# Two-layer attention decode: K and V in transfers of 32 KiB rows out of one planned arena

## The chip, the cores and the metric

One core of a Trainium2 chip runs the program. The metric is the device time of one execution in microseconds (us), here the median of three runs. TensorE (PE in the rows) multiplies, VectorE (DVE), ScalarE (ACT) and GpSimd (POOL) do the small work, and SyncE (SP) issues all transfers from HBM into the on-chip memory SBUF, which has 128 partitions. The transfers of one queue are carried by 16 DMA engines.

## The reference

Two different blocks are applied alternately, twice, to one token `x` of 512 elements. All is float32.

```python
def _A_ref(x, k_cache, v_cache, wq, wo):          # 32 heads, 4096 keys, 128 per head
    q = (x @ wq) as [1, 32, 1, 128]
    scores = einsum("bhqd,bhkd->bhqk", q, k_cache) * 128 ** -0.5
    p = softmax(scores)
    o = einsum("bhqk,bhkd->bhqd", p, v_cache)
    return o as [1, 1, 4096] @ wo

def _B_ref(x, w1, b1, w2, b2):                    # 512 -> 1376 -> 512
    return gelu(x @ w1 + b1) @ w2 + b2

x = x + _A_ref(layernorm(x), K, V, wq, wo)
x = x + _B_ref(layernorm(x), w1, b1, w2, b2)
x = x + _A_ref(layernorm(x), K, V, wq, wo)        # the same K, V and weights again
x = x + _B_ref(layernorm(x), w1, b1, w2, b2)
```

K and V have 64 MiB each, wq and wo 8 MiB each, w1 and w2 some 2.7 MiB each. Both layers read the same ones, and SBUF holds about a sixth of them, so nearly all of it is read twice.

## The kernel before

The 32 heads go in eight groups of four, one head of a group for each quadrant of the PE array. The 4096 keys of a group are cut into eight chunks of 512. A chunk of K (or of V) of one group is a tile of 128 partitions by 2048 elements: 8 KiB per partition, 1 MiB in all, and one transfer. wq and wo of a group have the same size.

Layer 0 takes the groups from 0 to 7, layer 1 from 7 to 0. For each group the program writes down, in this order:
- `scores`: eight chunks of K are fetched and multiplied with the queries (L158); 
- `query_block` and `queries`: wq of the next group is fetched and its queries are made (L145 to L152);
- `softmax` (L162 to L179);
- `values`: eight chunks of V are fetched and multiplied (L184);
- `head_out`: wo of the group is fetched, and the output of the heads is multiplied with it and added up in `pW` (L197).

After the eighth group `mlp` multiplies with w1 (L206), applies the GELU (L215 to L220) and multiplies with w2 in eleven blocks of 32 hidden units (L225). The mean and the variance of the layer norms come from small products with `negmean` (L126).

All tiles come from one pool, `ring`, of 25 buffers of 8 KiB per partition (`SLOTS`). `fetch` takes the next buffer and issues the transfer on SyncE's queue. A buffer is loaded anew when the engines have finished with its last content. In layer 0 the last 22 tiles (`KEPT`: K, V, wq and wo of group 7, wq and wo of group 6, and two chunks of V of group 6) stay in their buffers and are not fetched again in layer 1. A further chunk of V is copied to four free banks of PSUM (`pK`) and back (L78, L69). So layer 1 begins with work that needs no transfer.

Each transfer signals one of eight semaphores in turn, and SyncE issues a transfer when the one eight places before it has landed, so eight are in flight. The first three quarters of w1 (`w1_t`, 16,512 bytes of each partition, which lie 22,016 bytes apart in HBM) have a place of their own and are loaded once, before chunk 4 of the last V of layer 0. The rest of w1 (`w1_3`, rows of 1,376 bytes) and w2 in three parts go through the ring behind the last wo, in both layers. The last values of a layer are multiplied in the order 4, 0, 1, 2, 3, 5, 6, 7 (`ORDER`).

Of the kernel before, what the change touches and what calls it, by code (L numbers as in the profile page):

```python
# [12 lines left out]
F32 = mybir.dt.float32  # L13
# [14 lines left out]
SLOTS = 25           # streaming buffers of 8 KiB per partition  # L28
KEPT = 22            # buffers that stay filled from the first layer to the second
W1_AT = 4            # chunk of the last values before which w1 is loaded  # L30
MEAN_AT, VAR_AT = 0, 1   # parts of w1 whose products the mean and the variance follow
W2_PARTS = (3, 4, 4)     # blocks of 32 hidden units in each part of w2
ORDER = (4, 0, 1, 2, 3, 5, 6, 7)   # of the products with the last values: without
                                   # pauses, so that the tensor engine's clock is up
# [3 lines left out]
def decode_layers(ctx: ExitStack, tc: tile.TileContext, x, k, v, wq, wo, w1, b1, w2, b2, out):  # L38
    nc = tc.nc
    const = ctx.enter_context(tc.tile_pool(name="const", bufs=1))  # L40
    ring = ctx.enter_context(tc.tile_pool(name="ring", bufs=SLOTS))
# [8 lines left out]

    last = G - 1
    kept = [("k", last, c) for c in range(C)] + [("v", last, c) for c in range(C)]
    kept += [("wq", last), ("wo", last), ("wq", last - 1), ("wo", last - 1)]
    kept += [("v", last - 1, c) for c in range(C)]
    in_psum = kept[KEPT]
    kept = set(kept[:KEPT])
    held = {}

    def fetch(layer, what, *at):
        key = (what, *at)  # L60
        if key in held:
            return held.pop(key)
        src = dict(k=k, v=v, wq=wq, wo=wo)[what]
        for i in at:
            src = src[i]
        t = ring.tile([P, J, 512], F32, name="stream")
        if layer == 1 and key == in_psum:
            for j in range(J):
                nc.scalar.copy(t[:, j, :], pK[j])  # L69
            return t  # L70
        if key == ("wo", 0 if layer else last):
            for i in (0, 2):
                nc.sync.dma_start(t[:, i : i + 2, :], src[:, i : i + 2, :])
        else:
            nc.sync.dma_start(t, src)  # L75
        if layer == 0 and key == in_psum:
            for j in range(J):
                nc.scalar.copy(pK[j], t[:, j, :])  # L78
        if layer == 0 and key in kept:
            held[key] = t  # L80
        return t

# [3 lines left out]
    wq_next = fetch(0, "wq", 0)  # L86
    nc.sync.dma_start(b1c, b1)
    nc.sync.dma_start(b2c, b2)
    w1_t = ctile("w1_t", 3, J, FJ)

# [7 lines left out]
    # PSUM: four banks of products, and four that keep one more tile for the second layer.  # L98
    # Rows that no product writes are zero once and for all.
# [15 lines left out]
    # x and ones beside it: a product with both gives x W and the sums of W's columns.  # L115
# [85 lines left out]
    def mlp(xs, s, w1_3, w2_t):  # L201
        xb = small("xb", 4)
        nc.gpsimd.tensor_tensor(xb, xs[:, :, 0], b2c, op=ALU.add)  # L203
        for c in range(4):
            for j in range(J):
                nc.tensor.matmul(pH[32 * j : 32 * j + 2, :FJ], xs[:, c, :], w1_t[:, c, j, :] if c < 3 else w1_3[:, j, :FJ],  # L206
                                 start=(c == 0), stop=(c == 3))
# [113 lines left out]
```

## Time and profile before

| | |
|---|---|
| time of three runs | 701.38 us median (701.29 to 702.08) |
| span of the profiled execution, first to last instruction | 699.0 us |
| queue of SyncE | 287.19 MB, busy for 99.2% of 16 engines' span |
| mean rate | 412 GB/s |
| TensorE, weight load, VectorE, ScalarE busy | 63%, 12%, 11%, 3% |
| mean granted clock of TensorE | 0.73 |
| chain that ended last | DMA 86%, PE 10%, DVE 2% |

The span is 2.4 us shorter than the median of the runs, which also hold what lies ahead of the first and behind the last instruction. The share of the queue says how long its packets were under way on the 16 engines; it doesn't say that they ran at their best rate. The chain of waits is followed back from the last instruction; a piece of it that reads "DMA" is the time from the issue of a transfer to its landing, in which the transfers ahead of it in the queue are moved too. The granted clock is a share of TensorE's full 2.4 GHz, with 1.2 GHz (0.5) as the lower level.

### The profile page before, as it was taken

How to read it: one execution, taken by the hardware profiler on the slowest of the kernel's cores; microseconds unless marked ns; L12 is line 12 of the kernel's file. 1: busy time of each engine (PE TensorE's matmuls, PEld its weight loads, DVE VectorE, ACT ScalarE, POOL GpSimd, SP SyncE). 2: the span in 40 equal slices, each digit the busy share in tenths (PEclk: the TensorE clock that was granted, in tenths of full speed). 3: DMA queues.
4: the chain of work that ended last, by engine and by line, in shares of the span. 5: the costliest groups of instructions: out<-in, count | busy, mean ns of one | idle time of the engine just before them, and what ended most of it. 6: DMA issues, size and time to landing. Idle time of an engine off the chain costs nothing.

```text
span 699.0 us, 7892 instructions
## 1 busy us (share of the span) xinstructions
PE 440.4 (63%) x3440; PEld 87.3 (12%) x3440; DVE 77.8 (11%) x314; ACT 19.7 (3%) x43; POOL 3.5 (1%) x17
## 2 busy tenths in 40 slices
PE   4566666557656764666537887666767566665545
PEld 1010100001001010010003231101001001010012
DVE  2100101001001010010102120101001000010012
ACT  0100000000000000010000100000000000000000
POOL 0000000000000000000000000000000000000000
PEclk9676677876676568666659999765566756667768
DMA  8999999999999999999998999999999999999995
GB/s 340 420 422 421 420 421 420 422 421 420 421 421 422 420 421 421 420 422 420 424 418 327 417 421 420 421 421 421 421 422 420 423 420 423 420 421 423 421 418 228
DMA packets 41123, 287.70 MB, mean 412 GB/s; under 512 B 4992, under 2 KB 6016, under 8 KB 6784
## 3 DMA queue, kind: packets, MB, share of 16 engines
q1 hardware_dynamic: 41088, 287.19, 99.2%
q8 instruction: 27, 0.44, 0.3%
q14 instruction: 8, 0.07, 0.0%
HBM read 287.17 MB, written 0.00 MB: 411 GB/s over the span
## 4 chain that ended last, share of the span: by engine, by line
DMA 86%; PE 10%; DVE 2%; issue 1%; SPq 0%; ACT 0%; ACTq 0%; DVEq 0%
DMA stream<-in_v 40%; DMA stream<-in_k 27%; DMA stream<-in_wq 12%; DMA stream<-in_wo 6%; PE pO L184 5%; PE pS L158 2%; PE pB L197 1%; PE pA L225 1%; PE pB L206 1%; DMA stream<-in_w 1%; DVE wide L189 1%; SPq L75 0%; DVE mx L162 0%; PE pA L145 0%; DVE on L194 0%
## 5 line engine op out<-in xcount | busy, mean ns | idle before, releaser
L158 PE MATMUL pS<-stream,zq 128*8 128x512 f32 x1024 | 191.4, 837 | 90.9 <-DMA stream<-in_k 90.9
L184 PE MATMUL pO<-stream,pt 128*4 128x512 f32 x1024 | 173.5, 797 | 91.4 <-DMA stream<-in_v 86.2
L184 PEld LDWEIGHTS pO<-stream,pt 128*4 128x4 f32 x1024 | 21.8, 92 | 224.9 <-DMA stream<-in_v 155.4
L158 PEld LDWEIGHTS pS<-stream,zq 128*8 128x8 f32 x1024 | 18.6, 89 | 244.3 <-DMA stream<-in_k 232.2
L162 DVE TENSOR_REDUCE mx<-pS 128x1 f32<-128x512 f32 x16 | 11.1, 692 | 300.4 <-PE pS L158 300.4
L189 DVE STREAM_TRANSPOSE wide<-pO 128x512 f32<-128x512 f32 x16 | 11.5, 717 | 259.9 <-PE pO L184 259.9
L197 PE MATMUL pB<-stream,on 128*1 128x128 f32 x512 | 25.4, 361 | 20.0 <-DVE on L194 18.5
L171 PE MATMUL pO<-ident,wide 128*128 128x128 f32 x64 | 15.9, 396 | 31.2 <-ACT wide L169 31.2
L145 PE MATMUL pA<-stream,xs 128*2 128x128 f32 x512 | 24.4, 341 | 12.1 <-DMA stream<-in_wq 11.3
L169 ACT ACTIVATE wide<-pS,bias,sc 128x512 f32<-128x512 f32 x16 | 12.4, 777 | 580.2 <-DVE zq L152 485.7
L197 PEld LDWEIGHTS pB<-stream,on 128*1 128x1 f32 x512 | 14.3, 103 | 47.8 <-DVE on L194 43.5
L145 PEld LDWEIGHTS pA<-stream,xs 128*2 128x2 f32 x512 | 14.4, 100 | 35.4 <-DMA stream<-in_wq 28.4
L171 PEld LDWEIGHTS pO<-ident,wide 128*128 128x128 f32 x64 | 10.2, 195 | 39.0 <-ACT wide L169 35.7
L225 PE MATMUL pA<-stream,gelu_g 128*1 128x128 f32 x176 | 8.5, 372 | 4.5 <-DVE gelu_g L220 4.3
L225 PEld LDWEIGHTS pA<-stream,gelu_g 128*1 128x1 f32 x176 | 5.9, 111 | 7.7 <-DVE gelu_g L220 5.6
L150 DVE STREAM_TRANSPOSE wide<-pA 128x128 f32<-128x128 f32 x16 | 5.1, 316 | 11.5 <-PE pA L145 11.4
L175 DVE STREAM_TRANSPOSE mt<-ls 128x32 f32<-128x32 f32 x16 | 3.4, 211 | 17.5 <-ACT wide L169 17.5
L206 PE MATMUL pB<-w_t,xs 128*2 128x344 f32 x48 | 4.3, 450 | 1.4 <-DVE xs L120 1.4
L173 DVE COPY pt<-pO 128x128 f32<-128x128 f32 x16 | 4.5, 281 | 3.6 <-PE pO L171 3.6
L203 POOL TENSOR_TENSOR xb<-xs,b2c 128x4 f32<-128x4 f32 x2 | 0.4, 198 | 668.7 <-DVE xs L120 668.7
L166 DVE TENSOR_SCALAR mb<-m,nsc 128x8 f32<-128x8 f32 x16 | 3.7, 230 | 0.5
L194 DVE TENSOR_SCALAR on<-o,rl 128x4 f32<-128x4 f32 x16 | 3.7, 229 | 0.6
(68 smaller groups left out, 57.2 us busy)
## 6 DMA issues: line engine op xcount, KB each, us to landing
stream<-in_k SPq DMA_DIRECT2D x120, 1024.0 KB, 19.8
stream<-in_v SPq DMA_DIRECT2D x117, 1024.0 KB, 19.8
stream<-in_wq SPq DMA_DIRECT2D x14, 1024.0 KB, 19.8
stream<-in_wo SPq DMA_DIRECT2D x12, 1024.0 KB, 19.8
stream<-in_w SPq DMA_DIRECT2D x4, 1024.0 KB, 16.1
w_t<-in_w SPq DMA_DIRECT2D x1, 2064.0 KB, 22.3
stream<-in_wo SPq DMA_DIRECT2D x4, 512.0 KB, 19.3
stream<-in_w SPq DMA_DIRECT2D x2, 768.0 KB, 16.1
```

What stands on the lines that cost most here:

```text
L145: nc.tensor.matmul(pQ[32 * j : 32 * j + 2, :], xs[:, c, :], wt[:, c, P * j : P * (j + 1)], start=(c == 0), stop=(c == 3))
L150: nc.vector.transpose(qt, pQ)
L158: nc.tensor.matmul(pS[32 * j : 32 * j + C, :], z[:, j, C - 1 - c : 2 * C - 1 - c], kt[:, j, :], start=(c == 0), stop=(c == C - 1))
L162: nc.vector.tensor_reduce(mx[:, 0:1], pS, axis=AX.X, op=ALU.max)
L169: nc.scalar.activation(p, pS, AF.Exp, bias=bias[:, 0:1], scale=sc, accum_out=ls[:, 0:1])
L171: nc.tensor.transpose(pT[:, b].rearrange("p j r -> p (j r)"), p[:, P * b : P * (b + 1)], ident)
L173: nc.vector.tensor_copy(pt, pT[:, :, :, :C].rearrange("p b j c -> p j c b"))
L184: nc.tensor.matmul(pO[32 * j : 32 * j + 4, :], pt[:, j, c, :], vt[:, j, :], start=(i == 0), stop=(i == C - 1))
L189: nc.vector.transpose(ot[:, :512], pO)
L197: nc.tensor.matmul(pW[32 * j : 32 * j + 1, :], on[:, d : d + 1], wt[:, d, P * j : P * (j + 1)], start=first and d == 0, stop=final and d == 3)
L206: nc.tensor.matmul(pH[32 * j : 32 * j + 2, :FJ], xs[:, c, :], w1_t[:, c, j, :] if c < 3 else w1_3[:, j, :FJ], start=(c == 0), stop=(c == 3))
L225: nc.tensor.matmul(pM[32 * j : 32 * j + 1, :], g[:, c : c + 1], part[:, i, P * j : P * (j + 1)], start=(c == 0), stop=(c == FB - 1))
```

## The change

The ring is replaced by one tile, `arena`, of 27 places of 8 KiB per partition (216 KiB), and the program says for each transfer where in it the data goes (`load`). Every load is kept in the order of the program.

- K and V come in halves of four chunks: 128 rows of 32 KiB, 4 MiB per transfer. In HBM a half is stored so that a partition's four chunks are one run. The halves go round six blocks of four places in layer 0 and five in layer 1. Only the last V of each layer has its second half in four single chunks (`LAST`), and the first halves of layer 1 come in smaller pieces.
- wo and wq share one tensor `w` of two rows, in which wo of a group lies beside wq of a neighbour: one transfer of 128 rows of 16 KiB brings wo of this group and wq of the next into `PAIR`. The rows lie 64 KiB apart in HBM. The queries of the next group are therefore made after `head_out`, no longer before the softmax.
- w1 and w2 are loaded behind wo at the end of layer 0, each in two parts, to `HELD` and `SPARE`; the parts in `HELD` stay there, and layer 1 loads those in `SPARE` alone. wo of group 7 is a single load of 8 KiB rows.
- Kept from the first layer are K and V of group 7, wq and wo of group 7, and four chunks of V of group 6 (one by way of PSUM): 22 tiles. wq and wo of group 6 are fetched again. wq and two chunks of K of group 6 are loaded to `SPARE` when the products of layer 0 with w1 and w2 have been made.

```diff
+U = 512
+NC = 4 * U
+BLOCK = 4 * NC
+RING1, RING2 = 6, 5
+SPARE = 19 * NC
+HELD = 22 * NC
+PAIR = 25 * NC
+ARENA = 27 * NC
+W1H, W2A, W2B = 2 * FJ * J, 6 * U, 5 * U
+LAST = ((0, 4), (4, 5), (5, 6), (6, 7), (7, 8))
+HALVES = ((0, 4), (4, 8))
...
-        t = ring.tile([P, J, 512], F32, name="stream")
...
+    arena = const.tile([P, ARENA], F32, name="arena")
+    def load(at, src):
+        t = arena[:, at : at + src.shape[-1]]
+        tc.keep_in_program_order(nc.sync.dma_start(t, src))
         return t
...
+    def of_w(first, n):
+        row, i = first
+        return w[row][:, NC * i : NC * (i + n)]
...
+    def part(src, g, a, b):
+        h = a // 4
+        return src[g, h][:, NC * (a - 4 * h) : NC * (b - 4 * h)]
...
+    def stream(what, g, pieces, homes=None):
+        nonlocal block
+        src = k if what == "k" else v
+        for a, b in pieces:
+            if homes is not None:
+                at = homes[a]
+            else:
+                at = block * BLOCK + (a % 4) * NC
+                if b % 4 == 0:
+                    block = (block + 1) % ring
+            t = load(at, part(src, g, a, b))
+            for c in range(a, b):
+                here[what, g, c] = chunk(t, c - a)
+                yield c, here[what, g, c]
...
-            for c in range(C):
-                scores(z, c, fetch(layer, "k", g, c))
-            if not final:
-                wt = fetch(layer, "wq", order[n + 1])
...
+            if layer == 1 and n == 0:
+                tiles = [(c, here["k", g, c]) for c in range(C)]
+            elif layer == 1 and n == 1:
+                tiles = [(c, here["k", g, c]) for c in range(2)]
+                tiles += list(stream("k", g, ((2, 4), (4, 8)), {2: 0, 4: 2 * NC}))
+            else:
+                tiles = stream("k", g, HALVES)
+            for c, t in tiles:
+                scores(z, c, t)
...
             pt, rl = softmax(sc, nsc)
...
-                    if final and layer == 0 and len(vt) == W1_AT:
-                        nc.sync.dma_start(w1_t, w1[:, :3])
...
+            elif final:
+                tiles = dict(stream("v", g, LAST))
+                for i, c in enumerate(ORDER):
+                    values(i, pt, tiles[c], c)
...
+            elif final:
+                wo_t = chunk(load(PAIR + NC * layer, of_w(wo_at(g), 1)))
+                if layer == 0:
+                    load(HELD, w1[:, :W1H])
+                load(SPARE, w1[:, W1H:])
+                if layer == 0:
+                    load(HELD + W1H, w2[:, :W2A])
+                load(SPARE + W1H, w2[:, W2A:])
+            else:
+                t = load(PAIR, of_w(wo_at(g) if layer == 0 else wq_at(g - 1), 2))
+                wo_t, wq_next = (chunk(t, i) for i in ((0, 1) if layer == 0 else (1, 0)))
+            head_out(rl, wo_t, first, final)
+            if not final and not (layer == 1 and n == 0):
+                for c in range(4):
+                    query_block(c, xs, wq_next)
+                z = queries(n + 1, negm)
...
         if layer == 0:
             xs, s = set_x(of_32(mt, 4), 0.5, xb)
+            g = G - 2
+            wq_first = wq_next
+            wq_next = chunk(load(SPARE, of_w(wq_at(g), 1)))
+            for c in range(2):
+                here["k", g, c] = chunk(load(SPARE + NC * (c + 1), part(k, g, c, c + 1)))
```

Three places show how the order of the instructions changes. First SyncE's queue in a steady group of layer 0 (group 1), before and after; `in_w` is the common tensor of wq and wo in the changed kernel.

```order
L75 DMA stream<-in_k 128x2048 x8
L75 DMA stream<-in_wq 128x2048
L75 DMA stream<-in_v 128x2048 x8
L75 DMA stream<-in_wo 128x2048
L75 DMA stream<-in_k 128x2048 x8
```

```order
L62 DMA arena<-in_k 128x8192 x2
L62 DMA arena<-in_v 128x8192 x2
L62 DMA arena<-in_w 128x4096
L62 DMA arena<-in_k 128x8192 x2
L62 DMA arena<-in_v 128x8192 x2
```

Eighteen transfers of 1 MiB per group have become four of 4 MiB and one of 2 MiB, and wq has moved from between K and V to behind V.

Second, SyncE's queue from the last V of layer 0 into layer 1, with the semaphores that a transfer waits for (`DMAHW` are landings of earlier transfers, `PE` products that must be done). Here `in_w` is also the short name of w1 and w2, which the sizes tell apart. Before:

```order
L75 DMA stream<-in_v 128x2048 [waits DMAHW2_49,PE_49]
L73 DMA stream<-in_wo 128x1024 [waits DMAHW3_49,PE_49]
L73 DMA stream<-in_wo 128x1024 [waits DMAHW4_49]
L269 DMA stream<-in_w 128x4x344 [waits DMAHW5_49,PE_49]
L273 DMA stream<-in_w 128x1536 [waits DMAHW6_49,PE_49]
L273 DMA stream<-in_w 128x2048 [waits DMAHW7_49,PE_49]
L273 DMA stream<-in_w 128x2048 [waits DMAHW5_49,DMAHW0_49,PE_49]
L75 DMA stream<-in_k 128x2048 [waits DMAHW6_49,DMAHW1_49,PE_49]
L75 DMA stream<-in_k 128x2048 [waits DMAHW7_49,DMAHW2_49,PE_49]
```

And in the changed kernel:

```order
L62 DMA arena<-in_v 128x2048 [waits DMAHW5_49,PE_49]
L62 DMA arena<-in_w 128x2048 [waits DMAHW6_49,PE_49]
L62 DMA arena<-in_w 128x2752 [waits DMAHW7_49]
L62 DMA arena<-in_w 128x2752 [waits DMAHW0_49,Activation_49]
L62 DMA arena<-in_w 128x3072 [waits DMAHW1_49]
L62 DMA arena<-in_w 128x2560 [waits DMAHW2_49]
L62 DMA arena<-in_w 128x2048 [waits DMAHW3_49,DMAHW0_49,PE_49]
L62 DMA arena<-in_k 128x2048 [waits DMAHW4_49,DMAHW2_49,PE_49]
L62 DMA arena<-in_k 128x2048 [waits DMAHW5_49,PE_49]
L62 DMA arena<-in_k 128x4096 [waits DMAHW6_49,PE_49]
L62 DMA arena<-in_k 128x8192 [waits DMAHW7_49,PE_49]
```

All of w1 and w2 now stands behind the last wo, its parts wait for no product, and the first loads of layer 1 (wq, then K in pieces of 1, 1, 2 and 4 MiB) are the next that do.

Third, TensorE at the edge between groups 0 and 1, before (`L197` is the product with wo, `L145` the queries, `L158` the scores, `L184` the values):

```order
L158 MATMUL pS<-stream,zq_97 8x512 x32
L145 MATMUL pA<-stream,xs 2x128 x16
L171 MATMUL pO<-ident,wide 128x128 x4
L184 MATMUL pO<-stream,pt 4x512 x32
L197 MATMUL pB<-stream,on 1x128 x16
L158 MATMUL pS<-stream,zq_98 8x512 x32
```

And in the changed kernel, where the lines of the same products are L156, L143, L169, L182 and L195:

```order
L156 MATMUL pS<-arena,zq_91 8x512 x32
L169 MATMUL pO<-ident,wide 128x128 x4
L182 MATMUL pO<-arena,pt 4x512 x32
L143 MATMUL pA<-arena,xs 2x128 x13
L195 MATMUL pB<-arena,on 1x128 x16
L143 MATMUL pA<-arena,xs 2x128 x3
L156 MATMUL pS<-arena,zq_92 8x512 x32
```

The queries of the next group have moved from ahead of the transposes of the softmax to both sides of the product with wo.

## Rows read from the trace of the kernel before

**Rows 1.** The page: busy time, rate in 40 slices, packets, queue.
```profile
PE 440.4 (63%) x3440; PEld 87.3 (12%) x3440; DVE 77.8 (11%) x314; ACT 19.7 (3%) x43; POOL 3.5 (1%) x17
...
GB/s 340 420 422 421 420 421 420 422 421 420 421 421 422 420 421 421 420 422 420 424 418 327 417 421 420 421 421 421 421 422 420 423 420 423 420 421 423 421 418 228
DMA packets 41123, 287.70 MB, mean 412 GB/s; under 512 B 4992, under 2 KB 6016, under 8 KB 6784
...
q1 hardware_dynamic: 41088, 287.19, 99.2%
```

**Rows 2.** Chain that ended last: start, duration in us, what.
```profile
16.82 21.19 DMA stream<-in_v
...
38.03 19.88 DMA stream<-in_k
...
256.80 21.37 DMA stream<-in_wo
...
337.90 22.26 DMA stream<-in_v
...
375.23 4.77 DMA stream<-in_w
...
554.37 21.09 DMA stream<-in_wq
```

**Rows 3.** Transfers by what they load: count, KB each, us from issue to landing.
```profile
stream<-in_k SPq DMA_DIRECT2D x120, 1024.0 KB, 19.8
stream<-in_v SPq DMA_DIRECT2D x117, 1024.0 KB, 19.8
stream<-in_wq SPq DMA_DIRECT2D x14, 1024.0 KB, 19.8
stream<-in_wo SPq DMA_DIRECT2D x12, 1024.0 KB, 19.8
stream<-in_w SPq DMA_DIRECT2D x4, 1024.0 KB, 16.1
w_t<-in_w SPq DMA_DIRECT2D x1, 2064.0 KB, 22.3
```

**Rows 4.** Windows: busy us by engine, granted clock, DMA share, GB/s.
```profile
372.00:386.00 14.00, 10.38 (x204) 5.04 (x208) 4.11 (x25) 0.21 (x1) 1.44 (x5) 0.88 0.84 301
382.00:386.00 4.00, 3.32 (x68) 1.52 (x72) 1.56 (x12) 0.00 (x0) 0.55 (x1) 1.00 0.99 356
680.00:685.00 5.00, 3.84 (x36) 0.69 (x28) 1.02 (x3) 0.00 (x0) 0.00 (x0) 1.00 1.04 407
```

**Rows 5.** Timeline between the layers: start, us, engine, line, what, idle before.
```profile
367.87 0.10 PEld L184 LDWEIGHTS pO<-stream,pt 128*4 128x4 f32 x4 [0.33 <-DMA stream<-in_v]
...
372.36 0.76 PE L206 MATMUL pB<-w_t,xs 128*2 128x344 f32 x8 [0.64 <-DVE xs L120]
...
375.24 0.55 DVE L213 STREAM_TRANSPOSE wide<-pB 128x352 f32<-128x352 f32 x1 [1.02 <-PE pB L206]
...
377.30 2.55 PE L225 MATMUL pA<-stream,gelu_g 128*1 128x128 f32 x56 [2.14 <-DVE gelu_g L220]
...
380.05 1.70 PE L225 MATMUL pA<-stream,gelu_g 128*1 128x128 f32 x32 [0.19 <-DMA stream<-in_w]
...
384.39 7.05 PE L158 MATMUL pS<-stream,zq 128*8 128x512 f32 x64
```

**Rows 6.** Timeline behind the last chunk of V.
```profile
682.67 0.24 PEld L184 LDWEIGHTS pO<-stream,pt 128*4 128x4 f32 x8 [0.62 <-DMA stream<-in_v]
...
688.42 0.76 PE L206 MATMUL pB<-w_t,xs 128*2 128x344 f32 x8
...
691.91 4.25 PE L225 MATMUL pA<-stream,gelu_g 128*1 128x128 f32 x88 [2.15 <-DVE gelu_g L220]
```

**Rows 7.** Timeline at the start: queries, and scores of one chunk.
```profile
6.18 1.89 PE L145 MATMUL pA<-stream,xs 128*2 128x128 f32 x32 [1.37 <-DMA stream<-in_wq]
...
9.50 1.89 PE L158 MATMUL pS<-stream,zq 128*8 128x512 f32 x8 [1.43 <-DMA stream<-in_k]
```

More of the change, by code (lines that the diff above doesn't have):

```diff
@@ L49, in small, with chunk, wq_at, wo_at @@
         return work.tile([P, n], F32, name=name, bufs=2 if n < 32 else 1)
[L51 to L65, printed above, removed]
-        t = ring.tile([P, J, 512], F32, name="stream")
[L67 to L80, printed above, removed]
-        return t
+    arena = const.tile([P, ARENA], F32, name="arena")
+    def load(at, src):
+        t = arena[:, at : at + src.shape[-1]]
+        tc.keep_in_program_order(nc.sync.dma_start(t, src))
+        return t
+    def chunk(t, i=0):
+        return t[:, NC * i : NC * (i + 1)].rearrange("p (j n) -> p j n", j=4)
+    def of_w(first, n):
+        row, i = first
+        return w[row][:, NC * i : NC * (i + n)]
+    def wq_at(g):
+        return (g + 1) % 2, g
+    def wo_at(g):
+        return g % 2, g
+    def part(src, g, a, b):
+        h = a // 4
+        return src[g, h][:, NC * (a - 4 * h) : NC * (b - 4 * h)]
     b1c, b2c = ctile("b1c", FB), ctile("b2c", 4)
@@ L85, in decode_layers @@
     nc.sync.dma_start(xcol, x)
[L86 to L89, printed above, removed]
+    wq_first = chunk(load(HELD, of_w(wq_at(0), 1)))
     ident = ctile("ident", P)
@@ L234, in decode_layers @@
     xs, s = set_x(zero, 1.0, xcol)
+    nc.sync.dma_start(b1c, b1)
+    nc.sync.dma_start(b2c, b2)
+    here = {}
+    block = 2
+    def stream(what, g, pieces, homes=None):
[12 more added lines that the diff above has]
+                yield c, here[what, g, c]
+    w1_at = [HELD, HELD + FJ * J, SPARE, SPARE + FJ * J]
+    w2_at = [HELD + W1H + U * c if c < 6 else SPARE + W1H + U * (c - 6) for c in range(FB)]
+    w1_t = [arena[:, at : at + FJ * J] for at in w1_at]
+    w2_t = [arena[:, at : at + U] for at in w2_at]
     for layer in range(2):
+        ring = (RING1, RING2)[layer]
         order = list(range(G)) if layer == 0 else list(range(G))[::-1]
-        wt = wq_next if layer == 0 else fetch(1, "wq", order[0])
         for c in range(4):
-            query_block(c, xs, wt)
+            query_block(c, xs, wq_first)
             if c == 1:
@@ L255, in decode_layers @@
+            for c, t in tiles:
+                scores(z, c, t)
+            if layer == 1 and n == 0:
                 for c in range(4):
[L256 removed]
+                    query_block(c, xs, wq_next)
                 z = queries(n + 1, negm)
             pt, rl = softmax(sc, nsc)
[L259 to L265 removed]
@@ new lines, in decode_layers @@
+            if layer == 1 and n == 1:
+                block = 3
+            if layer == 1 and n == 0:
+                wo_t = chunk(arena[:, PAIR : PAIR + NC])
+            elif final:
[6 more added lines that the diff above has]
+                load(SPARE + W1H, w2[:, W2A:])
+            else:
+                t = load(PAIR, of_w(wo_at(g) if layer == 0 else wq_at(g - 1), 2))
+                wo_t, wq_next = (chunk(t, i) for i in ((0, 1) if layer == 0 else (1, 0)))
@@ L276, in decode_layers @@
+            head_out(rl, wo_t, first, final)
+            if not final and not (layer == 1 and n == 0):
+                for c in range(4):
+                    query_block(c, xs, wq_next)
+                z = queries(n + 1, negm)
         at = work.tile([P, P], F32, name="wide")
```

72 lines of the change are left out of this document (33 added, 39 removed).

## The prediction

> **What bounds the kernel now.** I read the page's slices first. The rate stands at 418 to 424 GB/s except in the first of 40 slices, in one past the middle and in the last [rows 1]. The queue of SyncE moves 287.19 MB and is busy for 99.2% of 16 engines' span, while the page gives TensorE 63%. So the time is that of the transfers, plus the places where their queue runs dry, plus a tail after the last K or V chunk.
>
> The chain of waits shows how the stream runs: eight transfers are in flight, and each link is a transfer that waits for the one eight places earlier. The link that starts at 38.03 and the one at 256.80 are eleven links, 88 transfers of 1 MiB, apart: 218.77 / 88 = 2.486 us each, of which I use 2.485; a link itself lasts 19.82 to 19.88, so some 0.05 us go by before the next issue counts [rows 2]. Three links are longer by 1.3 to 1.55 us (16.82, 256.80, 554.37). I carry these 4.2 us over unchanged.
>
> **What a longer row is worth.** The trace holds one transfer with longer rows: w_t, 2064 KB, 16,512 bytes per partition [rows 3]. First, is such a row one packet? Of 41,088 packets of the queue 6,784 are under 8 KB [rows 1], so 34,304 are not. The 263 stream transfers of K, V, wq and wo in 8 KiB rows (120 + 117 + 14 + 12) and four of w2 have 128 rows each [rows 3], 34,176; the remaining 128 are w_t's rows. So they went as one packet each.
>
> Its time: the link at 337.90 contains w_t and seven transfers of 1 MiB and lasts 22.26 us [rows 2]. With 0.05 us to the next issue that is 22.31 - 7 x 2.485 = 4.92 us. Each engine carries eight rows of a transfer (128 / 16), so a row of 8,192 bytes costs 2.485 / 8 = 310.6 ns and one of 16,512 costs 615 ns. The difference, 304.4 ns for 8,320 bytes, is 27.3 bytes per ns; at that pace 8,192 bytes need 300 ns, and some 10 ns are a cost per row. For 32 KiB I have no row, so I bound it:
> - at w_t's rate, with no further gain, 4 MiB take 4.92 x 4096 / 2064 = 9.76 us, 0.18 less than now (4 x 2.485 = 9.94);
> - with no cost per row at all, 8 x 32,768 / 27.3 = 9.60 us, 0.34 less;
> - with the same cost per row, 9.68 us, 0.26 less.
>
> The fit leans on a difference of two links that are read to 0.01 or 0.02 us, so I take a value between the first and the third, 9.72 us, **0.22 us less per 4 MiB**. Below nothing would need a mechanism that the trace doesn't show (a rival below).
>
> The Trainium skill has a price for a transfer as such ("DMA: Bandwidth & Descriptors", section "Anatomy of one DMA — SWDGE (gpsimd) path"): about 2.0 us fixed plus bytes / 436 GB/s, fitted on the software path. Taken as serial cost, three transfers fewer per block would save 6 us each, 336 us in all. The rows refuse this reading: transfers of 1 MiB follow each other every 2.485 us [rows 2], so the fixed part lies behind the others in flight.
>
> **The sum over the transfers.** By the program's order the changed kernel issues 56 transfers of 4 MiB, 14 of 2 MiB, 14 of 1 MiB, and parts of w1 and w2.
> - 56 x 0.22 = 12.3 us less.
> - 2 MiB in 16 KiB rows cost w_t's rate, 4.92 x 2048 / 2064 = 4.88 instead of 4.97: 14 x 0.09 = 1.2 us less.
> - The wo halves of 4 KiB rows, w1 in rows of 1,376 bytes and w2 in parts become rows of 8 to 12 KiB; for some 6 MiB I put down 0.3 us less.
> - One buffer fewer is kept. Ahead of the last V chunk the second layer fetches 121 MiB instead of 120 (wq and wo of group 6 come on top, V chunk 3 of it falls away): 2.5 us more. The parts of w1 and w2 that stay in the arena save bytes only behind the last V chunk, where the tail hides them.
>
> **The boundary between the layers.** Now the stream dips between 372 and 386: 301 GB/s over these 14 us against 421 lose 14 x 120 / 421 = 4.0 us [rows 4]. The loads of w2 and the next layer's K wait for buffers that TensorE still reads. A transfer put into an empty queue lands 4.77 us after its issue (the link at 375.23 [rows 2]), 2.3 us more than its own 2.485.
>
> In the changed kernel w1 and w2 go to places that are free by then, all after the last V chunk of layer 0. Call that chunk's landing T (367.87 now [rows 5]). Landings, with rows priced as above: wo T + 2.5, w1 T + 5.8 and T + 9.1, w2 T + 12.8 and T + 15.9. TensorE is ready for w1 at T + 4.5 (372.36), so it waits for each half: second half done at T + 10.7, GELU 2.1 us (375.24 to 377.30), first six blocks of w2 from T + 12.9 to 15.1, the last five until T + 17.8; the scores of layer 1 begin 2.6 us later, at T + 20.4 (now 381.75 to 384.39 [rows 5]). The queue: wq of group 6 can be issued from T + 10.7, hence no gap, landing T + 18.3. The first K chunk needs the place of w2's blocks 6 to 8, free at about T + 17.0, and lands at 17.0 + 2.3 + 2.5 = T + 21.8 instead of 20.8: 1.0 us lost. The next follows without a gap, at T + 24.3. The 2 MiB after it need the places of chunks 0 and 1 of the kept K: T + 20.4 + 2 x 0.88 (eight chunks in 7.05 us [rows 5]) = 22.2, landing T + 29.4, 0.2 lost. If TensorE runs those scores at its lower level (1.89 us for a chunk at the start [rows 7]) the loss here is 2.2; now the granted clock is 1.00 there [rows 4]. What follows (chunks 2 to 5 free at T + 25.7, V's places at about T + 35) is released in time. So 1.2 to 3.2 us are lost; I take 1.7, nearer the first, and so **2.3 us less than now**.
>
> **Steady groups.** The next load of a block has its turn in the queue five (in layer 1 four) blocks after the block's landing, 5 x 9.7 = 48 us or 39 us, and TensorE has finished it within some 15 us (8 chunks x 1.89 us [rows 7]). The pair wo and wq has one place: its next load waits for the query block, about 5 us after landing, with four blocks (39 us) queued in front of it. Moving the query block behind the output product puts 1.89 us of matmuls [rows 7] into a time when the next K block is still 9.7 us away. Hidden, all of it; uncovered it would cost 2.3 us for each empty queue.
>
> **The tail.** From the last V chunk (682.67) to the end of the span 16.3 us pass in dependent work: output product, w1 (its third part at 688.42), w2 at 691.91, the store [rows 6]. After the change wo lands behind that chunk as now, w1's second half 5.8 us and w2's 8.9 us after it; needed are these after 5.75 and (block 6, six times 0.39 past 691.91) 11.6 us. The first is level with its need; I add nothing.
>
> **Sum.** 699.0 - 12.3 - 1.2 - 0.3 + 2.5 - 2.3 = 685.4 us of span. The median of the runs, 701.38, is 2.4 us above the profiled span, which I keep: **687.8 us**, 1.9% less.
>
> **Rivals.**
> 1. *No gain per byte.* The 32 KiB rows are cut into 8 KiB pieces, or the 10 ns belong to bytes. For it: the trace shows no row above 16,512 bytes. Against it: those were not cut and ran faster. Then 699.0 + 2.5 - 2.3 - 0.3 + 2.4 = 701.3 us, no change. 7%.
> 2. *Rows that lie 32 KiB apart are read more slowly* (64 KiB for the pairs). Now the rows of a transfer lie back to back, 8 KiB apart, and w1's 22,016 bytes apart; a wide power of two is in no row. Price: the lowest rate of a window with a full queue is 407 GB/s (680 to 685 [rows 4]). At that rate 4 MiB take 10.31 us, and 56 x 0.37 = 20.7 us more, with nothing gained on the pairs: 722 us, slower. It decides from the point where K and V take back what the rest gives, 1.3 us: 9.94 + 1.3 / 56 = 9.96 us per 4 MiB. The skill's same page, section "Latency and other measured facts", reports copies between HBM tensors falling from a full 214 GB/s to 207 at 512 KiB between rows and to 103 at 4 MiB between rows. It says nothing of 32 and 64 KiB, and no run here shows it. 6%.
> 3. *Coarse blocks make the queue run dry.* SyncE's queue is in order, so one pair whose place is late holds every K block behind it. Each empty queue costs 2.3 us; at one per group 14 x 2.3 = 32 us, 685.4 + 32 + 2.4 = 720 us, slower. It decides from six of them on (13.6 / 2.3). Against it stand the 30 us and more of slack above. 5%.
>
> **How the numbers follow.** The forecast has 82%. Its own range: 0.18 to 0.34 us per block is 10 to 19 us, of which the lower two thirds are likelier; the boundary is uncertain by 2 us and the delays of single engines by 1.5: 684 to 692. Left out then are the rivals' 18%; to cover part of a half-realised rival I reach to 693.5. About 0.2% (1.4 us) can be told from no change here. Faster: the forecast and what lies between it and the first rival, 0.86; same: most of the first, 0.06; slower: the second, most of the third, 0.08.
>
> **What the next profile would show.** Right: links of the chain with 4 MiB steps of about 9.72 us, slices at 431 or 432 GB/s, a packet per row (some 13,500 in all with the small ones), the dip at the boundary shorter than 4 us, 16 us behind the last V chunk. Wrong: the rate still 421 (rival 1), near 407 (rival 2), or dips in every group with SyncE's queue waiting for TensorE (rival 3).

## The result, and the profile after

| | before | after |
|---|---|---|
| median of the runs | 701.36 us (701.29 to 702.08, 4 runs) | 690.05 us (689.26 to 691.14, 4 runs) |
| span of the profiled execution | 699.0 us | 689.0 us (its time: 690.76 us) |
| TensorE, weight load busy | 440.4, 87.3 us | 402.3, 106.9 us |
| mean granted clock | 0.73 | 0.77 |

The ratio is 0.9838 with a 95% interval of [0.9824, 0.9852]: 11.3 us less, where 13.6 were forecast. The time of 690.05 lies in the range, 2.25 us above the point.

The page of the changed kernel, the lines that answer to [rows 1]:

```profile
PE 402.3 (58%) x3440; PEld 106.9 (16%) x3440; DVE 77.6 (11%) x314; ACT 19.8 (3%) x43; POOL 3.6 (1%) x17
...
GB/s 345 432 435 427 431 432 431 427 432 430 431 431 423 439 430 431 431 424 437 420 422 332 417 435 433 429 432 425 434 435 431 432 427 425 436 432 433 427 413 143
DMA packets 13568, 287.84 MB, mean 418 GB/s; under 512 B 2016, under 2 KB 2016, under 8 KB 2016
...
q1 hardware_dynamic: 13536, 287.36, 97.7%
...
arena<-in_k SPq DMA_DIRECT2D x29, 4096.0 KB, 49.9
arena<-in_v SPq DMA_DIRECT2D x27, 4096.0 KB, 49.6
```

The typical slice is at 430 to 432 GB/s, as forecast, and no longer at 421. Packets fell from 41,123 to 13,568 (forecast: some 13,500), so a row of 32 KiB is one packet. The dip past the middle is still there, and the last slice is lower because the tail takes a larger share of it.

Four windows of the changed kernel: start and end, length, busy us of the engines, granted clock, DMA share, GB/s.

```profile
0.00:50.00 50.00, 23.28 (x172) 5.84 (x176) 6.41 (x33) 2.15 (x3) 1.37 (x10) 0.86 0.96 403
...
100.00:300.00 200.00, 109.57 (x870) 26.63 (x858) 18.91 (x71) 4.22 (x10) 0.00 (x0) 0.77 1.00 431
...
355.70:395.70 40.00, 30.65 (x401) 11.43 (x393) 8.21 (x41) 3.13 (x7) 1.44 (x5) 0.83 0.95 386
...
400.00:600.00 200.00, 118.75 (x970) 30.21 (x966) 21.29 (x80) 4.34 (x10) 0.00 (x0) 0.75 1.00 431
```

And the same of the kernel before:

```profile
0.00:50.00 50.00, 26.06 (x204) 5.11 (x204) 6.86 (x35) 2.15 (x3) 1.36 (x10) 0.83 0.96 392
...
100.00:300.00 200.00, 125.85 (x856) 19.07 (x848) 17.08 (x65) 3.47 (x8) 0.00 (x0) 0.71 1.01 421
...
367.90:407.90 40.00, 32.71 (x458) 13.00 (x454) 9.34 (x44) 3.02 (x7) 1.44 (x5) 0.91 0.96 379
```

What a stretch loses is its length times the missing share of the steady rate. The first 50 us lose 50 x (421 - 392) / 421 = 3.4 us before and 50 x (431 - 403) / 431 = 3.2 after: no change, as assumed. The 40 us behind the last V chunk of layer 0 lose 40 x 42 / 421 = 4.0 us before and 40 x 45 / 431 = 4.2 after, where I had forecast 1.7. In all the rest the stream runs at its steady rate. Most of the missing 2 us are there.

The chain of waits gives the steady rate more finely (start, duration, what):

```profile
101.03 48.74 DMA arena<-in_k
...
187.37 49.97 DMA arena<-in_k
...
276.33 49.95 DMA arena<-in_k
```

From the first to the last are four groups, 72 MiB: 175.30 / 4 = 43.83 us a group. Forecast were 4 x 9.72 + 4.88 = 43.76. Before, the 88 MiB between two links [rows 2] make 18 x 2.486 = 44.75 us. A group has become 0.92 us shorter, against 0.97 forecast. The two links between them give 43.17 and 44.48 us a group, so this is good to some tenths of a us only; by the windows it is 18 MiB at 421 and at 431 GB/s, 44.83 and 43.79 us, 1.04 less.

### The profile page after: what moved, and what is told of

It is laid out like the page before. It is cut to its first block, busy times and chain, and to the rows that moved or that the text cites. A ratio compares the mean times of both kernels' runs of the same rounds, so it can differ in the third digit from the quotient of the medians.

```text
span 689.0 us, 7523 instructions
## 1 busy us (share of the span) xinstructions
PE 402.3 (58%) x3440; PEld 106.9 (16%) x3440; DVE 77.6 (11%) x314; ACT 19.8 (3%) x43; POOL 3.6 (1%) x17
## 2 busy tenths in 40 slices
DMA packets 13568, 287.84 MB, mean 418 GB/s; under 512 B 2016, under 2 KB 2016, under 8 KB 2016
## 3 DMA queue, kind: packets, MB, share of 16 engines
q1 hardware_dynamic: 13536, 287.36, 97.7%
## 4 chain that ended last, share of the span: by engine, by line
DMA 63%; PE 22%; another core or an unknown queue 9%; DVE 3%; ACT 1%; issue 1%; SPq 0%; ACTq 0%; DVEq 0%
DMA arena<-in_k 36%; DMA arena<-in_v 18%; DMA arena<-in_w 10%; PE pO L182 10%; PE pS L156 9%; PE pA L221 1%; PE pB L195 1%; ACT wide L167 1%; PE pA L143 1%; DVE mx L160 1%; PE pO L169 1%; DVE wide L187 1%; SPq L62 0%; PE pB L204 0%
## 5 line engine op out<-in xcount | busy, mean ns | idle before, releaser
L156 PE MATMUL pS<-arena,zq 128*8 128x512 f32 x1024 | 173.0, 830 | 147.7 <-DMA arena<-in_k 147.7
L182 PE MATMUL pO<-arena,pt 128*4 128x512 f32 x1024 | 166.5, 810 | 65.7 <-DMA arena<-in_v 63.4
L156 PEld LDWEIGHTS pS<-arena,zq 128*8 128x8 f32 x1024 | 33.0, 112 | 275.0 <-issue 200.5
L182 PEld LDWEIGHTS pO<-arena,pt 128*4 128x4 f32 x1024 | 30.2, 104 | 190.9 <-issue 117.9
L169 PE MATMUL pO<-ident,wide 128*128 128x128 f32 x64 | 13.7, 350 | 44.8 <-ACT wide L167 44.8
L143 PE MATMUL pA<-arena,xs 128*2 128x128 f32 x512 | 22.7, 281 | 3.4 <-DMA arena<-in_w 2.6
L195 PE MATMUL pB<-arena,on 128*1 128x128 f32 x512 | 17.3, 272 | 8.9 <-DVE on L192 8.9
L169 PEld LDWEIGHTS pO<-ident,wide 128*128 128x128 f32 x64 | 8.8, 174 | 59.5 <-ACT wide L167 54.5
L143 PEld LDWEIGHTS pA<-arena,xs 128*2 128x2 f32 x512 | 14.8, 87 | 15.7 <-DMA arena<-in_w 6.7
L195 PEld LDWEIGHTS pB<-arena,on 128*1 128x1 f32 x512 | 11.8, 83 | 16.2 <-DVE on L192 15.4
L221 PE MATMUL pA<-arena,gelu_g 128*1 128x128 f32 x176 | 9.0, 396 | 4.3 <-DVE gelu_g L218 4.3
L204 PE MATMUL pB<-arena,xs 128*2 128x344 f32 x64 | 6.5, 529 | 2.4 <-DMA arena<-in_w 1.7
## 6 DMA issues: line engine op xcount, KB each, us to landing
arena<-in_k SPq DMA_DIRECT2D x29, 4096.0 KB, 49.9
```

Source lines behind the costliest of these rows:

```text
L143: nc.tensor.matmul(pQ[32 * j : 32 * j + 2, :], xs[:, c, :], wt[:, c, P * j : P * (j + 1)], start=(c == 0), stop=(c == 3))
L156: nc.tensor.matmul(pS[32 * j : 32 * j + C, :], z[:, j, C - 1 - c : 2 * C - 1 - c], kt[:, j, :], start=(c == 0), stop=(c == C - 1))
L169: nc.tensor.transpose(pT[:, b].rearrange("p j r -> p (j r)"), p[:, P * b : P * (b + 1)], ident)
L182: nc.tensor.matmul(pO[32 * j : 32 * j + 4, :], pt[:, j, c, :], vt[:, j, :], start=(i == 0), stop=(i == C - 1))
L195: nc.tensor.matmul(pW[32 * j : 32 * j + 1, :], on[:, d : d + 1], wt[:, d, P * j : P * (j + 1)], start=first and d == 0, stop=final and d == 3)
L221: nc.tensor.matmul(pM[32 * j : 32 * j + 1, :], g[:, c : c + 1], w2_t[c][:, P * j : P * (j + 1)], start=(c == 0), stop=(c == FB - 1))
```

## Experiments

The theory to test is that of the prediction: the gain is the row length alone, some 10 ns for each row of a transfer on its engine. Its rivals are that fewer and larger transfers bring it (a fixed part of each transfer), that the distance between the rows in HBM takes part, or that the planned places and the new order do. Each kernel ran beside the kernel before on the same chip.

**1. The same places and the same order, in rows of 8 KiB.** Only the transfers of K and V are cut; their data lie in HBM as in the changed kernel, so the rows are 32 KiB apart.

```diff
-            t = load(at, part(src, g, a, b))
+            t = arena[:, at : at + NC * (b - a)]
+            for c in range(a, b, 1):
+                load(at + NC * (c - a), part(src, g, c, min(c + 1, b)))
```

> The changed kernel, but each half of K or V comes as four transfers of 1 MiB in rows of 8 KiB, out of the same memory, in which the rows of a transfer begin 32 KiB apart, and to the same places. Theory R (a cost of some 10 ns per row): 0.22 us more per 4 MiB, 56 x 0.22 = 12.3 us, 702.4 us, and a step of 2.485 us per transfer. Rival: the gain came from the arena, its order and the boundary and not from the rows; then 690 us as in the changed kernel. If rows that begin 32 KiB apart are read more slowly than rows that lie back to back, this is over 703 us.

Measured: 701.64 us (701.18 to 703.02, 10 runs), ratio to the kernel before 1.000 [0.9991, 1.001]. One part undone gives back 11.6 us, all of the gain. The window of its steady stretch stands within 1 GB/s of the old rate:

```profile
100.00:300.00 200.00, 123.09 (x872) 22.87 (x864) 18.34 (x67) 3.48 (x8) 0.00 (x0) 0.70 1.01 422
```

So the arena, the order, the pairs and the further MiB bring, taken together, nothing of their own that can be measured. This run has shorter rows and also more transfers; experiment 3 tells the two apart.

**2. Rows of 16 KiB.** The loop of experiment 1 in steps of two chunks: transfers of 2 MiB.

> The changed kernel with each half of K or V as two transfers of 2 MiB in rows of 16 KiB. Theory R: twice 4.88 instead of 9.72 us per 4 MiB, 56 x 0.04 to 0.07 = 2 to 4 us more, 692 to 694 us. A cost per transfer alone (0.073 us each, so that three fewer give the 0.22) would make it 56 x 0.073 = 4.1 us more, 694 us; this run does not tell those two apart, the next one does.

Measured: 694.65 us (693.63 to 695.62, 4 runs), ratio 0.9901 [0.9884, 0.9918], and 428 GB/s in the same window:

```profile
100.00:300.00 200.00, 111.67 (x856) 23.15 (x860) 19.34 (x75) 4.35 (x10) 0.00 (x0) 0.79 1.01 428
```

The first doubling brings 7.0 us, the second 4.6. The 2 to 4 us expected for the second are narrowly missed. The cost per row found below (9.6 ns) would give 56 x 16 x 9.6 ns = 8.6 us for the first and 4.3 for the second.

**3. One transfer of 4 MiB, of 512 rows of 8 KiB.** K and V are stored chunk by chunk, and one instruction brings four chunks.

```diff
-        t = arena[:, at : at + src.shape[-1]]
-        tc.keep_in_program_order(nc.sync.dma_start(t, src))
+        if len(src.shape) == 3:
+            t = arena[:, at : at + NC * src.shape[0]]
+            d, src = t.rearrange("p (c n) -> p c n", n=NC), src.rearrange("c p n -> p c n")
+        else:
+            t = d = arena[:, at : at + src.shape[-1]]
+        tc.keep_in_program_order(nc.sync.dma_start(d, src))
...
-        return src[g, h][:, NC * (a - 4 * h) : NC * (b - 4 * h)]
+        return src[g, h][a - 4 * h : b - 4 * h]
```

> The changed kernel with as few transfers as it has, 4 MiB each, but K and V stored chunk by chunk, so that a transfer has 512 rows of 8 KiB. Theory R (cost per row): nearly all of the gain of the stream is gone, 56 x 0.20 = 11 us more, 701 us, a step of some 9.92 us per transfer. Rival T (cost per transfer, its completion): as the changed kernel, 690 us, a step of 9.72 us.

Measured: 702.50 us (701.79 to 703.26, 10 runs), ratio 1.0014 [1.0004, 1.0023]. The transfers are as large and as few as in the changed kernel, and nothing is gained:

```profile
100.00:300.00 200.00, 107.06 (x862) 26.57 (x854) 17.38 (x66) 3.47 (x8) 0.00 (x0) 0.78 1.01 422
```

The number of transfers is not the cause. The four rows of a partition land back to back in SBUF here as in the changed kernel, so it is the run in HBM that counts: the page has 35,168 packets on the queue, against 13,536.

The Trainium skill ("DMA: Bandwidth & Descriptors", section "Anatomy of one DMA — SWDGE (gpsimd) path") gives about 2.0 us fixed for each DMA on the software path. On this queue no such cost is paid one after the other, as the prediction held: transfers of 1 MiB (experiment 1) and of 4 MiB, both with rows of 8 KiB, move at the same 422 GB/s.

**4. Rows of 8 KiB that lie back to back in HBM.** The storage of experiment 3, with one transfer for each chunk.

> As the first of these four, four transfers of 1 MiB in rows of 8 KiB, but out of a memory in which the rows of a transfer lie back to back, as before the change. Theory R: the same as the first of the four, 702.4 us, within 1.5 us. Rival P (rows that begin 32 KiB apart cost something): faster than the first of the four by more than 1.5 us; the changed kernel would then hide a loss in its longer rows.

Measured: 702.34 us (701.58 to 703.31, 10 runs), ratio 1.0012 [1.0002, 1.0021], and again 422 GB/s in that window. Rows 32 KiB apart (experiment 1, 701.64 us) are not slower than rows without a gap; the 0.7 us between the two point the other way and lie within the 1.5 us expected. The rival of the wide distance falls for K and V.

**5. The boundary: spare parts first.** In the changed kernel the first loads of layer 1 wait until products with w1 and w2 have been made. Here those parts of w1 and w2 whose places are to be loaded anew come and are used first, and the second part of w2 comes in two pieces.

```diff
                 wo_t = chunk(load(PAIR + NC * layer, of_w(wo_at(g), 1)))
+                load(SPARE, w1[:, W1H:])
                 if layer == 0:
                     load(HELD, w1[:, :W1H])
-                load(SPARE, w1[:, W1H:])
+                load(SPARE + W1H, w2[:, W2A:])
                 if layer == 0:
-                    load(HELD + W1H, w2[:, :W2A])
-                load(SPARE + W1H, w2[:, W2A:])
+                    load(HELD + W1H, w2[:, : 4 * U])
+                    load(HELD + W1H + 4 * U, w2[:, 4 * U : W2A])
...
-        mt, xb = mlp(x1, s1, w1_t, w2_t)
+        a, b = list(range(6)), list(range(6, FB))
+        mt, xb = mlp(x1, s1, w1_t, w2_t, (0, 1, 2, 3) if layer else (2, 3, 0, 1), a + b if layer else b + a)
```

(Left out: the lines in `mlp` that take the two new orders of the parts.)

> The changed kernel, in which layer 0 loads and multiplies the parts of w1 and w2 in the spare places first (before those that are kept), and its last part of w2 in pieces of four and two blocks. Theory: at the boundary the queue runs dry because the first loads of layer 1 wait for the products with w2's last part, which lies in their places; with these products done before the last part lands, wq and the first two K chunks of layer 1 follow without a gap. The first K chunk lands 20.8 instead of 22.3 us behind the last V chunk of layer 0, and the time falls by 1 to 2 us, to 688.5. Rival: what is lost there is the delay of single engines by other transfers, which the order doesn't touch; then 690 us.

Measured: 690.72 us (688.89 to 692.34, 5 runs), ratio 0.984 [0.982, 0.986]: no gain. Windows of the changed kernel at the boundary:

```profile
368.00:372.00 4.00, 2.58 (x52) 1.79 (x56) 0.92 (x5) 0.21 (x1) 0.00 (x0) 0.50 0.86 320
372.00:376.00 4.00, 3.25 (x84) 2.10 (x76) 0.83 (x6) 0.00 (x0) 0.00 (x0) 0.77 0.50 170
376.00:380.00 4.00, 3.81 (x47) 1.13 (x48) 0.91 (x7) 0.00 (x0) 0.55 (x1) 1.00 1.12 434
```

And of this kernel:

```profile
372.00:376.00 4.00, 3.27 (x64) 1.95 (x60) 0.49 (x3) 0.00 (x0) 0.00 (x0) 0.50 0.95 360
376.00:380.00 4.00, 3.36 (x60) 1.46 (x52) 1.23 (x9) 0.00 (x0) 0.55 (x1) 0.60 0.49 203
```

The dip to 170 is gone from its place and comes back 4 us later, at 203. Over the 40 us behind the last V chunk this trace moves 370 GB/s, where the changed kernel has 386; it is the trace of the slowest of the five executions (692.34 us):

```profile
356.00:396.00 40.00, 30.34 (x380) 11.19 (x373) 8.21 (x41) 3.13 (x7) 1.44 (x5) 0.74 0.90 370
```

Its waits of SyncE between 366 and 400 us (total, times, longest):

```profile
SPq L62 <- PE pS L156: 11.1, 2, 8.0
...
SPq L62 <- PE pA L221: 3.5, 2, 3.0
```

In the changed kernel these are 7.2 us for the scores (`pS`), 4.1 the longest, and 2.3 us for w2's products (`pA`). The first K chunk does land 20.9 us behind the last V chunk, as expected (356.08 to 376.94, the landings in the trace). The load that was released earlier now stands in front of the next, which needs the place of a kept K chunk; TensorE reads that no earlier than before (its scores start at 378.09 instead of 376.81 us), since all of w1 and w2 has to land first. A wait was moved, not removed.

**6. The two bias loads later.** The small loads of b1 and b2 are moved from ahead of the first group's K to behind it.

```diff
-    nc.sync.dma_start(b1c, b1)
-    nc.sync.dma_start(b2c, b2)
...
+            if layer == 0 and first:
+                tc.keep_in_program_order(nc.sync.dma_start(b1c, b1))
+                tc.keep_in_program_order(nc.sync.dma_start(b2c, b2))
             pt, rl = softmax(sc, nsc)
```

> The changed kernel, in which the two small transfers of the biases are issued behind the first group's K and not ahead of it. Theory S: the first half of K lands 1.3 us later than four chunks landed before because its long rows start beside the short ones of the biases; without them it lands at 16.4 instead of 17.6 us and the time falls by up to 1.2 us. Rival: the first rows of a stream are slow whatever is ahead of them; then no difference.

Measured: 689.83 us (688.72 to 690.62, 4 runs), ratio 0.983 [0.9813, 0.9847]. In the trace the first scores start at 15.89 instead of 17.77 us, and the first 50 us run at 408 instead of 403 GB/s, worth 50 x 5 / 431 = 0.6 us. The runs show 0.2 us, within their scatter: the gain is not told apart from nothing by the runs. The traces speak for theory S: the first 50 us run at 408 GB/s in all four with this edit (6, 8, 9 and 11) and at 401 to 404 in the four without it (the changed kernel, 5, 7 and 10).

**7. The pairs as two transfers of 8 KiB rows.** K and V stay at 32 KiB.

```diff
-                t = load(PAIR, of_w(wo_at(g) if layer == 0 else wq_at(g - 1), 2))
+                row, i = wo_at(g) if layer == 0 else wq_at(g - 1)
+                load(PAIR, of_w((row, i), 1))
+                load(PAIR + NC, of_w((row, i + 1), 1))
+                t = arena[:, PAIR : PAIR + 2 * NC]
```

> The changed kernel with wo and wq of a pair in two transfers of 8 KiB rows, which begin 64 KiB apart as the rows of 16 KiB do. By the cost per row 14 x 0.09 = 1.2 us more, 691.3 us. If the pair's rows were slowed by their distance, or if a pair's landing mattered for the queries, more than 1 us would show in either direction.

Measured: 689.69 us (689.55 to 691.1, 4 runs), ratio 0.9834 [0.9817, 0.9851]. The 1.2 us that the sum gives to the pairs are not seen in the times; with runs that scatter over 1.5 us they are not excluded either. The rate shows them:

```profile
400.00:600.00 200.00, 117.71 (x966) 29.56 (x962) 20.72 (x80) 4.34 (x10) 0.00 (x0) 0.77 1.00 429
```

The seven traces with whole pairs and K and V in rows of 32 KiB have 430 to 432 in this window. The rounding goes away when the bytes of each packet in the trace are spread over the packet's own time: from 60 to 320 us it is 429.9 GB/s here and 430.6 in each of the seven. For a group of 18 MiB that is 0.07 us, in 14 groups 1.0 us, near the 1.2 of the sum.

**8. Experiments 5 and 6 together.**

> The first two of these four together. If both theories hold the gains add up, 687.5 us, 0.4% below the changed kernel; if neither does, 690 us.

Measured: 689.70 us (687.85 to 690.86, 4 runs), ratio 0.9827 [0.9806, 0.9848]: no measurable difference to either.

**9. Half of w1 before the last half of V.** If the wait is only moved because all of w1 and w2 must land behind the last V chunk, one part has to come earlier. The spare half of w1 finds its place free by then. On top of experiment 8:

```diff
-                tiles = dict(stream("v", g, LAST))
+                tiles = dict(stream("v", g, LAST[:1]))
+                if layer == 0:
+                    load(SPARE, w1[:, W1H:])
+                tiles.update(stream("v", g, LAST[1:]))
...
-                load(SPARE, w1[:, W1H:])
-                if layer == 0:
+                if layer == 1:
+                    load(SPARE, w1[:, W1H:])
+                else:
```

> The combined kernel of the last run, in which the spare half of w1 is also loaded ahead of the last V's second half in layer 0. Theory: with the first K chunks no longer late, the boundary is now bound by the scores of the kept K, whose places the next 2 MiB need, and these by the chain through w1 and w2; with half of w1 there ahead of the last V chunk the chain waits for one half of w1 only, ends about 1.5 us earlier in the stream, and the 2 MiB land some 29 instead of 31 us behind the same point. The time falls by 1 to 2 us against the combined kernel, to 688. Rival: TensorE, which waits more before and has less work at a stretch, runs the scores at its lower level and the wait stays; then 689.5 us.

Measured: 688.61 us (688.08 to 689.19, 5 runs), ratio 0.9819 [0.9805, 0.9832]. That is 1.1 us under experiment 8, the expected way, but the runs of the two overlap. The 40 us behind the last V chunk or close to it, in experiment 8 and here:

```profile
354.50:394.50 40.00, 30.68 (x401) 11.87 (x397) 8.23 (x41) 3.13 (x7) 1.44 (x5) 0.83 0.94 389
...
355.00:395.00 40.00, 32.47 (x437) 12.17 (x433) 8.54 (x42) 3.13 (x7) 1.43 (x5) 0.91 0.97 400
```

At 431 that is 3.9 us lost and 2.9.

**10 and 11. The changed kernel and the version of experiment 9 side by side.** Their intervals overlapped, so both ran again on one chip.

> The changed kernel as it is, beside the version with the early half of w1, on one chip. It gave 690.05 us. If the three edits of that version are worth what the windows say (the stream loses 2.9 instead of 4.2 us between the layers) it stays at 690.0 +- 0.6 us; if the difference was chance between chips, it comes within 0.5 us of the other.

> The version with the early half of w1 again: 688.6 +- 0.5 us, 1.4 us below the changed kernel of the same chip, if its gain is real; within 0.5 us of it if the gain was chance.

Measured: 690.29 us (689.91 to 691.30, 4 runs) for the changed kernel, 688.38 us (687.66 to 689.38, 5 runs) for version 9; ratios to the kernel before 0.9845 [0.9831, 0.9858] and 0.982 [0.9806, 0.9833]. On this chip every run of version 9 is shorter than every one of the changed kernel: 1.9 us between the medians, against 1.4 in the first runs. Windows of the changed kernel in this run, the start and the 40 us behind the last V chunk:

```profile
0.00:50.00 50.00, 22.91 (x176) 5.88 (x180) 6.40 (x33) 2.15 (x3) 1.36 (x10) 0.90 0.97 404
...
355.00:395.00 40.00, 29.87 (x404) 11.28 (x400) 8.32 (x41) 3.13 (x7) 1.44 (x5) 0.87 0.95 391
```

And of version 9:

```profile
0.00:50.00 50.00, 23.16 (x168) 5.40 (x172) 6.30 (x33) 2.15 (x3) 1.36 (x10) 0.90 0.97 408
...
355.00:395.00 40.00, 32.31 (x477) 12.72 (x473) 9.34 (x44) 3.13 (x7) 1.44 (x5) 0.98 0.99 407
```

At 431 the boundary loses 3.7 us here and 2.2 in version 9, the start 0.5 us more here: 2.0 us together, near the 1.9 between the medians. Version 9 is the fastest that was run. It holds the edits of experiments 5 and 6 too; how the 1.9 us divide among the three was not run side by side.

## Why the prediction was right, and where its sizes were off

**Row length: right.** Experiment 3 undoes the row length alone, with as few transfers as in the changed kernel, and gives back all of the gain (702.50 us); experiment 1 does so with more transfers. With 16 engines the rates 421 (the kernel before), 428 (experiment 2) and 431 GB/s are 311.3, 612.5 and 1216.4 ns for a row of 8, 16 and 32 KiB. A straight line through the first and the last gives 301.7 ns for 8 KiB and 9.6 ns for each row; it puts the middle one at 613.0. The 9.6 is good to about 1 ns: the rates are rounded, and a ninth of the changed kernel's bytes, the pairs, comes in rows of 16 KiB. The packets of the traces say the same by themselves: their median time is 312 ns for 8 KiB (the kernel before), 614 for 16 KiB (experiment 2) and 1215 for 32 KiB.

The prediction had 300 and 10 from a single transfer of 16,512-byte rows. Of its three bounds for 4 MiB the chain now gives (43.83 - 4.88) / 4 = 9.74 us if the pair cost 4.88: between "no further gain" (9.76) and the value taken (9.72). Before, 4 MiB took 9.94 us by the chain [rows 2] and 9.96 at 421 GB/s. So the gain is 0.20 to 0.22 us per 4 MiB where 0.22 were forecast; the readings do not tell these apart.

**Pairs, w1 and w2 rows, the further MiB.** Together 1.0 us more in the sum (2.5 - 1.2 - 0.3). Experiment 1 bears on them only in sum with the boundary: with K and V in 8 KiB rows the rest of the change comes to nothing measurable. The pairs are seen in the rate (experiment 7). The rows of w1 and w2 and the further MiB were not settled by themselves.

**The boundary: the step that failed.** The prediction took 2.3 us less loss. It put the first K chunk of layer 1 at "T + 21.8 instead of 20.8: 1.0 us lost", let the next follow "without a gap", and lost 1.7 us in all. The waits were named rightly, their size was not: by the windows 4.2 us are lost (3.7 in experiment 10), so the term is about 0. The timeline of the changed kernel (start, us, idle before):

```profile
364.79 2.47 PE L204 MATMUL pB<-arena,xs 128*2 128x344 f32 x16 [1.66 <-DMA arena<-in_w]
...
369.42 4.73 PE L221 MATMUL pA<-arena,gelu_g 128*1 128x128 f32 x88 [2.17 <-DVE gelu_g L218]
...
373.49 9.05 SPq L62 DMA_DIRECT2D arena<-in_k  x4
...
376.81 7.05 PE L156 MATMUL pS<-arena,zq 128*8 128x512 f32 x64
```

Was the chain of products through w1 and w2 late? A transfer has landed when the last of the 16 engines is done with it, and the trace holds these times: T, the landing of the last V chunk, is 355.66. w2's products end at T + 18.5 (forecast 17.8) and the scores begin at T + 21.1 (20.4), each 0.7 us late; the products with the second half of w1 took 2.47 us, at a granted clock of 0.50 (window 364.5 to 367.5). In experiment 10, the same kernel with T at 355.69, they took 1.50:

```profile
364.86 1.50 PE L204 MATMUL pB<-arena,xs 128*2 128x344 f32 x16 [1.98 <-DMA arena<-in_w]
...
371.59 1.80 PE L221 MATMUL pA<-arena,gelu_g 128*1 128x128 f32 x40 [0.23 <-DMA arena<-in_w]
...
376.04 7.05 PE L156 MATMUL pS<-arena,zq 128*8 128x512 f32 x64
```

Both marks came as forecast there, at T + 17.7 and T + 20.4, and yet 3.7 us were lost. So the chain's time was not what the sum had wrong. The landings show what was:

| transfer | lands after T: forecast | measured | experiment 10 | gap ahead of it, mean of 16 engines: measured, experiment 10 |
|---|---|---|---|---|
| second half of w1 | 9.1 | 9.1 | 9.1 | none |
| last part of w2 | 15.9 | 15.8 | 15.9 | none |
| wq | 18.3 | 18.3 | 18.3 | 0.7, 0.3 |
| first K chunk | 21.8 | 22.3 | 21.9 | 2.8, 3.0 |
| second K chunk | 24.3 | 26.3 | 25.8 | 0.2, 0.2 |
| the 2 MiB of K | 29.4 | 31.2 | 30.7 | 0.5, 0.2 |

(A gap is the time between the landings of two transfers, averaged over the engines, less the transfer's own time at the steady rate.) Without any gap the second K chunk would land at T + 23.3. Ahead of the two K chunks 1.0 us of loss was forecast; measured are 3.0 and 2.5 on the last engine, and 3.0 and 3.1 on the mean of the engines. In the rate it is the dip from 368 to 376, 4 x (111 + 261) / 431 = 3.5 us.

The forecast followed the last landing as if the 16 engines were level. They are not: at T the first engine is done at 351.62 and the last at 355.66, 4.0 us apart; at the first K chunk all are done within 0.24 us. The early engines had run dry while the last one still worked, and the sum has no term for that. It also set 1.7 us, counted from last landings, against the 4.0 us of before, which come from a rate and so from all engines. What spreads the engines, and what makes the last engine of the second K chunk late, is not shown.

Experiments 5 and 9 show which release helps: letting wq and the first K chunks go earlier only shifts the dip, and loading half of w1 ahead of V shortens it (2.9 and 2.2 us in two traces). The higher end of the forecast's loss, scores at a lower clock, did not come: they ran at a granted 1.00 in 7.05 us. The 1.89 us a chunk that the prediction took for the lower level [rows 7] carries no mark of it either: the profile's clock column reads 1.00 from 9.50 to 11.40.

**Steady groups: right.** SyncE waits for TensorE's scores far longer in sum than before (total, times, longest; first the kernel before):

```profile
SPq L75 <- PE pS L158: 5.6, 9, 1.5
...
SPq L62 <- PE pS L156: 147.6, 28, 6.7
```

Yet the rate is 431 in the long windows: the third rival's wait exists, with blocks queued ahead of it. The chain of waits now shows TensorE with 22% of the span instead of 10%, and another 9% without a name. The steady rate says that this is no new bound.

**The tail.** Timeline of the last steps:

```profile
671.32 0.10 PEld L182 LDWEIGHTS pO<-arena,pt 128*4 128x4 f32 x4 [0.41 <-DMA arena<-in_v]
...
685.62 0.35 SPq L344 DMA_DIRECT2D out<-y  x1
```

From the last V chunk to the issue of the store 14.30 us pass; before it was 14.1 (682.67 [rows 6] to 696.77). The weights behind V are in time, as forecast. But the store lands 2.4 us after its issue, not 1.4. The same store took 1.4 us in the traces of experiments 1, 3, 4 and 7 and 2.3 to 3.0 in those of 2, 5, 6 and 8 to 11. What decides it is open.

**The way from span to median.** I added 2.4 us to the span as a fixed part. The runs that list both have 1.7 to 1.9 us (690.76 against 689.0; the same in the kernel before, 701.0 against 699.2). The other 0.6 us were that the profiled execution of before was shorter than its median; the profiled one of after is 0.7 us longer than its own. In spans of profiled executions the change is 10.0 us, in medians 11.3. Of the 3.6 us that the span misses of its 13.6, 2.2 lie ahead of the last V chunk (671.32 instead of 682.67 - 13.6 = 669.07), where the boundary is, and 1.4 behind it.

The rivals: "no gain per byte" fell with the rate of 431, "rows that lie 32 KiB apart" with experiments 1 and 4, "coarse blocks" with the long windows. For the pairs, whose rows lie 64 KiB apart, the packets speak: a row of 16 KiB took 613 ns there (median, the changed kernel) and 614 in experiment 2, where most lie 32 KiB apart.

## What to carry to other kernels

Where a queue is full all the time, count its rows and not its transfers: here each cost some 10 ns on its engine, so a layout in HBM that makes four rows one is worth 2% of the time at 8 KiB, and the next doubling less than the one before. A stall between two stages is priced by the rate of its window, with every place that the next loads need followed back to the product that frees it. A landing is that of the last engine; the others may stand dry long before it, so a loss from last landings and a loss from a rate are two measures. Here a stall of several links in one chain got shorter when the chain started earlier, and only moved when its first links alone were released. Before a term of 1 or 2 us is believed or denied, compare medians, or both versions side by side: single executions of this kernel scatter by 2 us.

## What the hardware showed that was not expected

TensorE got faster without a change in its work: 402.3 us busy instead of 440.4 for the same 3440 matmuls, the granted clock 0.77 instead of 0.73. The size of the transfers takes part in that, at the same rate of the stream: in experiments 1 and 4, with chunks that land one by one, it was 423.2 and 421.6 us and a clock of 0.73 to 0.76 in all runs, in experiment 3, with four chunks at once, 401.6 us and 0.77 to 0.78. That longer stretches of work without a pause raise the clock is argued from this and not shown; two chunks at once (experiment 2) had the highest of all, 0.80. To the time it brought nothing: experiment 3 has the faster TensorE and takes 702.50 us, since the stream sets the time.

A row of 32 KiB goes as one packet: 13,536 on the queue, against 37,872 in experiment 1. With blocks of 4 MiB a transfer takes 49.9 us from issue to landing instead of 19.8 [rows 3], and the stream is faster all the same: the time to landing says how much stands in the queue, not how fast it moves.
